# A fused attention and gated-MLP kernel whose instruction order is rehearsed: counting only whole operands for a shared port, with the table of places searched anew

## The chip, the cores and the metric

The kernel runs on one core of one Trainium2 chip. The metric is the device time of one execution in microseconds (us); lower is better. The median of several executions is compared with that of the other kernel.

## What is computed

Eight batches, each with eight attention heads over 576 positions of width 64, and behind them one gated MLP per batch (model width 512, inner width 1024).

```python
scores = 0.125 * q @ k.T
keep   = scores >= max(scores) - tau          # per row
attn   = where(keep, exp(scores - max), 0);  attn /= sum(attn) + 1e-9
x      = heads side by side of attn @ v       # (8, 576, 512)
h      = gelu_tanh(x @ w_in);  u, v = halves of h
v_n    = layer_norm(v) * g_ln
v_s    = einsum('ts,bsd->btd', w_sg, v_n) + b_sg
out    = x + (u * v_s) @ w_out
```

## The kernel before, in words

The heads are handled two at a time. A "pair" n (0 to 31, four to a batch) has nine score tiles of 128 rows by 576 columns: tiles i = 0 to 3 for each head h, and one tile (i = 4, buffer `pm`) that holds the last 64 rows of both heads. Products that need float32 accuracy are made of two parts in a 22-bit format, a high part and a rest, so a score tile is four matmuls against `ks` (high) and `klz` (rest) with `qst`.

For each score tile the engines work in a chain. TensorE writes the scores to PSUM (L785; L767 for the first pair), VectorE takes the negated row maximum (L794, `nm`), GpSimd makes the threshold from it (L800, one column), ScalarE the exponentials (L820, `p`), VectorE then selects and sums (L827: one instruction that reads the scores from PSUM, the threshold column and `p`), TensorE transposes `p` (L535) and ScalarE places the result (L905, L924). The product with `v` is L935. A batch's four pairs give `x`, and only then its MLP matmuls (all of them L1035) can run. They are fed by ScalarE, VectorE and GpSimd through GELU, statistics (L1101, L1104) and splits (L1136, L1196); at the end GpSimd adds the residual (L1223) and SyncE stores.

The weights `w_in` and `w_out` arrive as float64 and are made float32 on the chip, in twelve blocks of 128 rows by 512 columns. A block is loaded by SyncE (L564, `raw_wi` or `raw_wo`, 512 KB), and then takes one ScalarE operation (L572), five VectorE operations (L577, L579, L581, L583, L589) on scratch tiles `wt` or `wz`, and GpSimd and ScalarE operations (L591, L595, L598). These five are called *weight operations* below; there are 60 of them. Blocks `wi01` to `wi31` are the half of `w_in` that the first MLP matmuls need.

SyncE's queue carries all transfers, in order: loads of q, k and v (`rq`, `rk`, `rv`), the weights, and the copies inside SBUF that put a pair's parts in their places (`qst`, L724; `ks`, L702; `klz`, L710; the two `ks` tiles of a pair are `ks<n>_0` and `ks<n>_1`).

The order of all this isn't written by hand. The kernel's body runs twice. The first time it runs against a `Planner` that only records each operation with its engine, an assumed duration and its needs. Each step has a place, `time + scale * OFF[kind] + START[group]`, and `order()` rehearses the program: on each engine, of the steps that could start within `LOOK[engine]` ns of the earliest, the one with the lowest place is taken. The order so found is then issued on the chip, where it is fixed for each engine. One rule of the rehearsal concerns a port that VectorE and GpSimd share: a VectorE operation that is recorded with more than one port (`ports > 1`) starts only after GpSimd's running operation, and holds GpSimd back until it ends itself. These are the lines of it:

```python
if e == "vector" and ops[k][5]:
    if turn["gpsimd"] < start < free["gpsimd"]:
        start = free["gpsimd"]
    turn[e] = start + ns
elif e == "gpsimd":
    start = turn[e] = max(start, turn["vector"])
```

Of the kernel before, what the change touches and what calls it, by code (L numbers as in the profile page):

```python
# [30 lines left out]


OFF = dict(
    tau=-3286.52, q_tails=4436.42, w_load=9629.26, w_abs=4070.14, w_word=-12546.53, w_mul=9713.12, w_add=1259.24,
    w_hi=13076.7, w_lo=-3653.97, w_cast=-4392.8, w_rest=-5913.28, w_place=-8284.37, q_load=4520.75, q_scale=-2406.12,
    q_hi=2053.6, q_lo=-14065.23, q_place=6174.73, q_place_lo=-1344.24, k_load=6900.96, k_hi=430.25, k_lo=10089.47,
    k_place0=9510.54, k_place1=-7562.99, l_place0=-1744.14, l_place1=-1468.81, v_load=11820.02, s=-2160.62,
    nm=5825.84, thr=3055.12, exp=-6580.43, stt=4998.09, t=5700.02, hi=-2640.78, rep=2476.92, tt=119.62, thi=-10085.17,
    guard=-514.64, recip=-6412.4, irep=3638.48, turn=710.41, inv=7549.47, pv=8049.18, rmul=-8520.37, xh=533.49,
    xl=-6641.52, pe=8140.36, msq=-6600.8, stt1=-3927.08, tanh=5227.1, stt2=-2470.89, bn=-4656.45, ag=-8321.5,  # L40
    var=7088.56, rstd=-389.91, shift=3242.69, vn=-2579.53, z=5969.97, zh=-13084.52, zl=-1807.31, mg=-2328.37,
    mgh=3292.78, mgl=454.79, mo=-5098.92, mxl=6386.64, mxh=-6162.46, mst=-19677.21, mlow=-1641.06, madd=5763.85,
    xt=-6497.96,
)
START = {
# [10 lines left out]
}  # L56
LAST_SCALE, SIGMA, SPREAD = 0.55, 1.155, 0.7
LOOK = dict(tensor=20.8, vector=91.4, scalar=115.7, gpsimd=100.2, sync=4015.6)

# [13 lines left out]
    tensor=dict(tensor=0, vector=196, scalar=197, gpsimd=224, sync=190),  # L73
    vector=dict(tensor=230, vector=127, scalar=128, gpsimd=155, sync=120),
    scalar=dict(tensor=260, vector=146, scalar=153, gpsimd=170, sync=135),
    gpsimd=dict(tensor=205, vector=68, scalar=68, gpsimd=100, sync=67),
    sync=dict(tensor=1180, vector=907, scalar=978, gpsimd=983, sync=900),
# [8 lines left out]
def time_of(engine, op, out, args):  # L86

    n = out.size // out.shape[0]
    pointers = sum(a.size == a.shape[0] for a in args) if n > 1 else 0
    args = args or [out]  # L90
    half = out.shape[0] < P and n < 512
    if op == "memset":
        return n / 1.2 + (175 if engine == "gpsimd" and half else 35)
    if engine == "tensor":
        passes = 2 if op == "transpose" else 4 if args[0].dtype == F32 else 1
        beside = 0.5 if min(out.shape[0], args[0].shape[0]) < P and n < 512 else 1.0
        return n * passes * beside / (CLOCK if passes > 1 else STREAM) + (2 if beside == 1 else 20)
    if engine == "scalar":
        return n / 1.2 + (51 if args[0].psum else 93) + 93 * pointers + 115 * half
    if engine == "vector":  # L100
        fast = op == "tensor_scalar" and not args[0].psum
        if op == "tensor_reduce":
            n = args[0].size // args[0].shape[0]
        elif op == "bn_stats":
            n = args[0].size // args[0].shape[0]
        return n / (1.92 if fast else 0.96) + 69 + (60 if pointers else 0)
    if engine == "gpsimd":
        if n == 1 and op == "tensor_tensor":
            return 464 if pointers else 150
        if len(out.shape) == 4:  # L110
            return 149 + n + 140
        return 149 + n * (1.0 if op == "tensor_scalar" else 2.103) + (115 if half or 1 < n < 8 else 0)
    if out.tile.dram:
        return out.size * 0.44
    return out.size * (4 if n >= P else 8) / DMA_BYTES
# [52 lines left out]
class Planner:  # L168
# [51 lines left out]
    def _record(self, engine, op, out, args, accum_out, kw):  # L220
        reads = [a for a in (*args, *kw.values()) if isinstance(a, View)]
        writes = [a for a in (out, accum_out) if isinstance(a, View)]
        me, needs = len(self.ops), {}

        def touch(t):
            self.before[self.current].add(t.step)
            if t.ring:
                ring, k, bufs = t.ring
                if k >= bufs:
                    self.replaced.append((needs, ring[k - bufs]))  # L230

        done = []
        for view, write in [(v, False) for v in reads] + [(v, True) for v in writes]:
            t, (p0, p1, cols) = view.tile, view.area()
            found, rest = False, []
            for j, other, q0, q1, c in t.past:
                meets = q0 < p1 and p0 < q1 and c & cols
                if meets and (write or other) and j != me:
                    found = True
                    needs[j] = needs.get(j, False) or not write  # L240
                if not (write and p0 <= q0 and q1 <= p1 and not c & ~cols and self.ops[j][0] != self.current):
                    rest.append((j, other, q0, q1, c))
            if not found:
                touch(t)
            t.past = rest
            done.append((t, (me, write, p0, p1, cols)))
        for t, entry in done:
            t.past.append(entry)
            t.users[me] = True
        first = writes[0] if writes else reads[0]  # L250
        ports = sum(not a.psum for a in reads) + (op == "tensor_scalar" and not reads[0].psum)
        self.ops.append((self.current, engine, time_of(engine, op, first, reads), needs,
                         P if engine == "tensor" else first.shape[0], engine == "vector" and ports > 1,
                         engine == "tensor" and op != "transpose" and args[0].dtype == F32
                         and min(first.shape[0], args[0].shape[0]) < P))
# [26 lines left out]
    def order(self):  # L282
# [86 lines left out]
        def choose(e):  # L369
# [7 lines left out]
            if starts:  # L377
                soonest = min(starts.values()) + LOOK[e]
                i = min((i for i, t in starts.items() if t <= soonest), key=lambda i: (self.place[i], i))
# [926 lines left out]
```

## Time and profile before

| | |
|---|---|
| median of 3 runs (lowest, highest) | 1009.51 us (1008.3, 1011.13) |
| profiled execution: time, span from first to last instruction | 1008.32 us, 1006.5 us |
| TensorE matmul busy | 966.0 us, 96% of the span |
| VectorE, ScalarE, GpSimd busy | 670.3, 694.3, 622.1 us |
| mean granted TensorE clock | 0.989 |
| moved by DMA | 96.43 MB, mean 96 GB/s |

The page's second part cuts the span into 40 slices of about 25 us. TensorE's digits there begin with 5, 6, 8, 8 and are 9 from the fifth slice to the last but one; VectorE's are 6, 8, 9, 9, 9 in the first five and mostly 6 or 7 after that. A row's "busy" time is the union of its instructions; successive instructions of one engine overlap a little in the records, so that start-to-start distances are shorter than durations. A bracket at the end of a timeline row gives the idle time of the engine before it and what ended it.

### The profile page before, as it was taken

To read this page: it belongs to the slowest core of one execution; us is meant where nothing else is said; L and a number is where in the kernel's file an instruction comes from. 1 tells how busy PE (TensorE), PEld (TensorE's weight loads), DVE (VectorE), ACT (ScalarE), POOL (GpSimd) and SP (SyncE) were. 2 spreads that over 40 slices of the span, in tenths; PEclk is the share of its full clock that TensorE was granted. 3 is DMA by queue.
4 is the path that set the end of the run, shared out by engine and by line. 5 is a ranking of instruction groups with operands and counts; after the bars stand their busy time and mean duration, and the time that the engine had idled before them with its cause. 6 is when DMAs were issued, how large, how long until landed. Compare 5 with 4: busy or idle time off the path is not lost.

```text
span 1006.5 us, 20067 instructions
## 1 busy us (share of the span) xinstructions
PE 966.0 (96%) x6940; PEld 834.5 (83%) x6940; DVE 670.3 (67%) x1419; ACT 694.3 (69%) x1485; POOL 622.1 (62%) x1109
## 2 busy tenths in 40 slices
PE   5688999999999999999999999999999999999997
PEld 4566778898798978889788987889878897889887
DVE  6899988674777657674677746777386755674251
ACT  4678888675778568674786747776577756875362
POOL 4678788557655576555764567555765557634557
PEclk9789999999999999999999999999999999999999
DMA  7855444243134522344133540355223451220001
GB/s 218 252 146 142 114 107 111 67 119 97 43 96 117 140 56 77 94 122 122 32 95 89 143 112 21 87 131 128 80 53 97 113 134 55 71 52 24 24 1 48
DMA packets 50759, 96.43 MB, mean 96 GB/s; under 512 B 8033, under 2 KB 16225, under 8 KB 50658
## 3 DMA queue, kind: packets, MB, share of 16 engines
q1 hardware_dynamic: 50658, 95.15, 35.8%
q8 instruction: 55, 0.90, 0.4%
q14 instruction: 46, 0.38, 0.1%
HBM read 38.44 MB, written 9.44 MB: 48 GB/s over the span
## 4 chain that ended last, share of the span: by engine, by line
PE 70%; POOL 9%; ACT 7%; DMA 5%; DVE 4%; issue 3%; SPq 1%; POOLq 0%; ACTq 0%; DVEq 0%
PE all_banks L1035 35%; PE all_banks L785 13%; PE all_banks L535 11%; PE all_banks L935 11%; POOL z L1136 2%; POOL vv L1123 2%; ACT pt L905 1%; ACT vv L1120 1%; DVE p L827 1%; POOL bn L1112 1%; DMA wt<-in_w_sgT 1%; ACT z L1129 1%; POOL x L953 1%; DMA qst<-qhi 1%; ACT p L820 1%
## 5 line engine op out<-in xcount | busy, mean ns | idle before, releaser
L794 DVE TENSOR_REDUCE nm<-all_banks 128x1 f32<-128x576 f32 x288 | 215.1, 752 | 74.6 <-PE all_banks L785 63.0
L827 DVE SCALAR_TENSOR_TENSOR p<-all_banks,nm,p 128x576 f32<-128x576 f32 x256 | 205.3, 813 | 74.0 <-POOL nm L800 42.5
L820 ACT ACTIVATE p<-all_banks,nm 128x576 f32<-128x576 f32 x256 | 188.2, 744 | 31.3 <-DVE nm L794 30.1
L785 PE MATMUL all_banks<-ks,qst 128*128 128x288 f32 x620 | 189.2, 323 | 8.9 <-DMA ks<-khi 5.1
L905 ACT ACTIVATE pt<-all_banks 128x512 f32<-128x512 f32 (+1 forms) x320 | 169.2, 557 | 24.2 <-PE all_banks L535 22.5
L535 PE MATMUL all_banks<-ident_r,p 128*128 128x128 f32 x1152 | 174.8, 281 | 11.4 <-DVE p L827 8.9
L785 PE MATMUL all_banks<-klz,qst 128*128 128x288 f32 x620 | 174.1, 298 | 0.1
L535 PEld LDWEIGHTS all_banks<-ident_r,p 128*128 128x128 f32 x1152 | 138.1, 144 | 26.5 <-DVE p L827 12.5
L785 PEld LDWEIGHTS all_banks<-ks,qst 128*128 128x128 f32 x620 | 118.3, 191 | 36.0 <-issue 16.9
L935 PE MATMUL all_banks<-pt,rv 128*64 128x320 f32 (+1 forms) x1024 | 138.3, 412 | 0.2
L1035 PE MATMUL all_banks<-x,wi 128*128 128x288 f32 (+2 forms) x768 | 120.4, 299 | 0.0
L785 PEld LDWEIGHTS all_banks<-klz,qst 128*128 128x128 f32 x620 | 118.9, 192 | 1.4 <-DMA klz<-rk 0.6
L800 POOL TENSOR_TENSOR nm<-columns,nm 128x1 f32<-128x1 f32 x288 | 60.5, 217 | 91.3 <-DVE nm L794 87.0
L1035 PE MATMUL all_banks<-wsh,z 128*128 128x288 f32 (+2 forms) x512 | 115.2, 300 | 0.3 <-ACT z L1129 0.3
L1223 POOL TENSOR_TENSOR ot<-ot,x 128x288 f32<-128x288 f32 (+2 forms) x128 | 102.6, 806 | 14.4 <-ACT ot L1220 9.2
L1035 PE MATMUL all_banks<-gh,wo 128*128 128x288 f32 (+2 forms) x512 | 111.5, 300 | 0.0
L1035 PE MATMUL all_banks<-wi,x 128*128 128x512 f32 x448 | 109.3, 393 | 0.4 <-DVE uu L1014 0.4
L935 PEld LDWEIGHTS all_banks<-pt,rv 128*64 128x64 f32 x1024 | 67.8, 136 | 50.4 <-issue 8.2
L1035 PEld LDWEIGHTS all_banks<-x,wi 128*128 128x128 f32 x768 | 106.2, 188 | 0.8 <-issue 0.5
L1035 PEld LDWEIGHTS all_banks<-wi,x 128*128 128x128 f32 x448 | 80.2, 184 | 18.1 <-DVE uu L1014 0.8
L1035 PEld LDWEIGHTS all_banks<-wsh,z 128*128 128x128 f32 x512 | 85.0, 188 | 0.6 <-ACT z L1129 0.5
L1196 POOL TENSOR_TENSOR gl<-uu,gh 128x288 fp32r<-128x288 f32 (+2 forms) x64 | 51.2, 804 | 54.2 <-ACT gh L1192 53.5
(169 smaller groups left out, 1731.3 us busy)
## 6 DMA issues: line engine op xcount, KB each, us to landing
rk<-in_kT SPq DMA_DIRECT2D x32, 320.0 KB, 3.1
rv<-in_vP SPq DMA_DIRECT2D x32, 320.0 KB, 3.0
ks<-khi SPq DMA_DIRECT2D x62, 160.0 KB, 2.6
rq<-in_qT SPq DMA_DIRECT2D x32, 288.0 KB, 3.1
qst<-qhi SPq DMA_DIRECT2D x62, 144.0 KB, 3.2
qst<-rq SPq DMA_DIRECT2D x62, 144.0 KB, 2.4
ks<-khi SPq DMA_DIRECT2D x62, 144.0 KB, 2.5
out_T<-ot SPq DMA_DIRECT2D x56, 144.0 KB, 1.8
```

Of the source, the lines that this page charges most:

```text
L535: nc.tensor.transpose(out, x, ident_r.bitcast(F32))
L785: nc.tensor.matmul(sc[:, a, 0:HALF], w, x, start=(j == 0), stop=(j == len(terms) - 1))
L794: nc.vector.tensor_reduce(nmax, st["s", h, i][:, :, 0:HALF], AX.XY, ALU.max, negate=True)
L800: nc.gpsimd.tensor_tensor(thr, toff, st["nm", h, i], ALU.subtract)
L820: nc.scalar.activation(target(h, i), st["s", h, i][:, :, 0:HALF], AF.Exp, bias=st["nm", h, i])
L827: nc.vector.scalar_tensor_tensor(dst, st["s", h, i][:, :, 0:HALF], st["thr", h, i], dst, ALU.is_ge, ALU.mult, accum_out=st["l", p][:, c:c ...
L905: nc.scalar.activation(dst, src, AF.Copy)
L935: nc.tensor.matmul(acc[h * D:(h + 1) * D, 0:w], st["v"][:, o:o + D], unit(h, p)[:, kt, 0:w] if kt < NM else tail_unit(p)[:, 0:w], start=(k ...
L1035: nc.tensor.matmul(st["acc"][0:rows[0]] if rows else st["acc"], w, x, start=(j == 0), stop=(j == n - 1))
L1123: nc.gpsimd.tensor_tensor(st["v", i], st["v", i], g_bc[0:rows], ALU.mult)
L1196: nc.gpsimd.tensor_tensor(st["gl", p, d], st["u", p, d], st["gh", p, d], ALU.subtract)
L1223: return lambda: nc.gpsimd.tensor_tensor(o(), o(), x[b, m][:, ts_], ALU.add)
```

## The change

Three things are edited. The line that counts an operation's SBUF operands for the port now leaves out operands of one element per partition (columns such as a threshold). By the old line the select (L827: threshold column and `p` from SBUF) counted two ports, by the new one it counts one. The weight operations, and the GELU operations of a batch's last 64 rows (L1014, L1020), count two by either. The numbers in `OFF`, `START` and `LOOK` are all replaced; `LOOK` for SyncE goes from 4015.6 to 49883.6 ns, for GpSimd from 100.2 to 250.5, for TensorE from 20.8 to 109.7. No operation is added, removed or resized.

```diff
-    tau=-3286.52, q_tails=4436.42, w_load=9629.26, w_abs=4070.14, w_word=-12546.53, w_mul=9713.12, w_add=1259.24,
...
+    tau=-13072.53, q_tails=17013.18, w_load=24017.7, w_abs=10671.59, w_word=11608.84, w_mul=22204.76, w_add=6419.5,
...
-LOOK = dict(tensor=20.8, vector=91.4, scalar=115.7, gpsimd=100.2, sync=4015.6)
+LOOK = dict(tensor=109.7, vector=84.7, scalar=108.3, gpsimd=250.5, sync=49883.6)
...
-        ports = sum(not a.psum for a in reads) + (op == "tensor_scalar" and not reads[0].psum)
+        ports = sum(not a.psum and a.size > a.shape[0] for a in reads) + (op == "tensor_scalar" and not reads[0].psum)
```

What this moves is seen in the built programs. Names carry the pair and the tile (`p4_0` is `p` of pair 4, tile 0) and a serial number that differs between the two.

SyncE's queue in the opening, before: the stretch that ends in the copies for pair 1's second `ks` tile.

```order
L685 DMA rk2_265<-in_kT 128x640
L564 DMA raw_wi30_272<-in_w_in 128x1024
L564 DMA raw_wi01_281<-in_w_in 128x1024
L564 DMA raw_wi11_288<-in_w_in 128x1024
L564 DMA raw_wi21_292<-in_w_in 128x1024
L564 DMA raw_wi31_297<-in_w_in 128x1024
L564 DMA raw_wo0_311<-in_w_out 128x1024
L564 DMA raw_wo1_313<-in_w_out 128x1024
L564 DMA raw_wo2_320<-in_w_out 128x1024
L702 DMA ks1_1_338<-khi1_228 64x640 x2
```

The same engine after the change, the stretch up to the same copies.

```order
L564 DMA raw_wi30_156<-in_w_in 128x1024
L724 DMA qst01_115<-qhi1_162 64x576
L724 DMA qst11_117<-qhi1_162 64x576
L724 DMA qst01_115<-rq1_138 64x576
L724 DMA qst11_117<-rq1_138 64x576
L702 DMA ks1_0_243<-khi1_231 64x576 x2
L710 DMA klz10_124<-rk1_143 64x640
L685 DMA rq2_268<-in_qT 128x576
L710 DMA klz01_123<-rk1_143 64x576
L702 DMA ks1_1_296<-khi1_231 64x640 x2
L685 DMA rk2_315<-in_kT 128x640
```

In the first, eleven of the twelve weight loads stand ahead of `ks1_1` in the queue (three of them ahead of the rows shown); in the second four do, and `rv0` and `rv1`, which stood ahead, now follow.

VectorE in the opening, before: from the first select of pair 1's tile 0 to the next maxima of its second head.

```order
L827 SCALAR_TENSOR_TENSOR p1_0_370,l1_0_371<-all_banks_91,nm1_0_0_363,p1_0_370 128x576
L579 TENSOR_SCALAR wz0_349<-wz0_349 128x512
L794 TENSOR_REDUCE nm1_0_1_410<-all_banks_91 128x1
L843 RECIPROCAL l0_1_277<-l0_1_277 128x5
L581 SCALAR_TENSOR_TENSOR wz0_349<-raw_wi01_281,wz0_349 128x512
L589 SCALAR_TENSOR_TENSOR wt3l_245<-raw_wi20_183,wt3l_245 128x512
L577 TENSOR_SCALAR wt4h_422<-wt4h_422 128x512
L583 TENSOR_SCALAR wz0_349<-wz0_349 128x512
L579 TENSOR_SCALAR wt4h_422<-wt4h_422 128x512
L827 SCALAR_TENSOR_TENSOR p1_1_419,l1_0_371<-all_banks_91,nm1_0_1_410,p1_1_419 128x576
L581 SCALAR_TENSOR_TENSOR wt4h_422<-raw_wi30_272,wt4h_422 128x512
L794 TENSOR_REDUCE nm1_1_0_455<-all_banks_91 128x1
```

VectorE after the change, from the same select on.

```order
L827 SCALAR_TENSOR_TENSOR p1_0_355,l1_0_356<-all_banks_91,nm1_0_0_337,p1_0_355 128x576
L843 RECIPROCAL l0_1_261<-l0_1_261 128x5
L827 SCALAR_TENSOR_TENSOR p1_0_355,l1_0_356<-all_banks_91,nm1_1_0_374,p1_0_355 128x576
L946 TENSOR_TENSOR x32_0_0_408<-all_banks_91,ir0_0_238 128x256
L794 TENSOR_REDUCE nm1_0_1_417<-all_banks_91 128x1
L583 TENSOR_SCALAR wt3l_205<-wt3h_204 128x512
L579 TENSOR_SCALAR wt4h_376<-wt4h_376 128x512
L589 SCALAR_TENSOR_TENSOR wt3l_205<-raw_wi20_153,wt3l_205 128x512
L794 TENSOR_REDUCE nm1_0_2_447<-all_banks_91 128x1
L794 TENSOR_REDUCE nm1_1_1_459<-all_banks_91 128x1
L827 SCALAR_TENSOR_TENSOR p1_1_453,l1_0_356<-all_banks_91,nm1_0_1_417,p1_1_453 128x576
```

The weight operations that stood between the two selects of that tile have moved behind them. Counted from the programs' starts, 52 weight operations stand ahead of the second select of pair 4's tile 0 before and 46 after, with 38 selects and 39 maxima ahead in both; up to the last select of pair 3's tile 3 it is 51 and 44.

TensorE around the transposes of pair 4's tile 0, before.

```order
L535 MATMUL all_banks_91<-ident_r_92,p4_0_1177 128x128 x4
L535 MATMUL all_banks_91<-ident_r_92,ir3_1_1219 128x128 x2
L535 MATMUL all_banks_91<-ident_r_92,l3_1_1060 128x128
L785 MATMUL all_banks_91<-ks4_1_1087,qst10_116 128x288
L785 MATMUL all_banks_91<-klz10_124,qst10_116 128x288
L785 MATMUL all_banks_91<-ks4_1_1087,qst10_116 128x288
L785 MATMUL all_banks_91<-klz10_124,qst10_116 128x288
L535 MATMUL all_banks_91<-ident_r_92,p4_0_1177 128x128 x5
```

TensorE after the change, at the same place.

```order
L1035 MATMUL all_banks_91<-wi11_1069,x1_693 128x512 x3
L1035 MATMUL all_banks_91<-wi21_1159,x2_942 128x512 x2
L785 MATMUL all_banks_91<-ks4_1_1108,qst10_116 128x288
L785 MATMUL all_banks_91<-klz10_124,qst10_116 128x288
L785 MATMUL all_banks_91<-ks4_1_1108,qst10_116 128x288
L785 MATMUL all_banks_91<-klz10_124,qst10_116 128x288
L1035 MATMUL all_banks_91<-wi21_1159,x2_942 128x512
L1035 MATMUL all_banks_91<-wi31_1168,x3_1184 128x512 x3
L535 MATMUL all_banks_91<-ident_r_92,p4_0_1143 128x128
L535 MATMUL all_banks_91<-ident_r_92,ir3_1_1239 128x128 x2
L535 MATMUL all_banks_91<-ident_r_92,l3_1_1052 128x128
L535 MATMUL all_banks_91<-ident_r_92,p4_0_1143 128x128 x4
```

Twelve MLP matmuls of the first batch (three stand just ahead of the rows shown) now come before the second half of these transposes; before, the first of them comes some 50 rows after these.

More of the change, by code (lines that the diff above doesn't have):

```diff
@@ L33 @@
 OFF = dict(
-    tau=-3286.52, q_tails=4436.42, w_load=9629.26, w_abs=4070.14, w_word=-12546.53, w_mul=9713.12, w_add=1259.24,
[L35 to L43, printed above, removed]
+    tau=-13072.53, q_tails=17013.18, w_load=24017.7, w_abs=10671.59, w_word=11608.84, w_mul=22204.76, w_add=6419.5,
+    w_hi=10498.51, w_lo=-13326.63, w_cast=9980.35, w_rest=-4899.43, w_place=-2267.44, q_load=4326.97, q_scale=4377.77,
+    q_hi=-2442.43, q_lo=-12231.14, q_place=30436.83, q_place_lo=1664.62, k_load=10334.3, k_hi=-6857.66, k_lo=-685.55,
+    k_place0=-19333.51, k_place1=-3297.61, l_place0=24572.89, l_place1=-14784.81, v_load=58431.42, s=-30373.95,
+    nm=13996.8, thr=-3490.07, exp=18012.16, stt=18418.78, t=-1553.44, hi=6288.69, rep=20685.74, tt=-6558.4,
+    thi=2889.11, guard=-2787.69, recip=-3700.6, irep=-995.86, turn=-5627.14, inv=30071.87, pv=18033.85,
+    rmul=-18400.62, xh=12547.41, xl=-45570.85, pe=4060.27, msq=-202.81, stt1=19882.23, tanh=-4905.84, stt2=-19666.94,
+    bn=-16580.9, ag=-14071.83, var=-3342.04, rstd=21481.31, shift=19191.57, vn=5742.16, z=15012.34, zh=-12985.82,
+    zl=-11826.14, mg=-6619.76, mgh=23319.86, mgl=-3933.56, mo=20106.66, mxl=28163.49, mxh=-20280.11, mst=-31173.79,
+    mlow=-19270.9, madd=8715.79, xt=-19524.59,
 )
 START = {
[10 rows of a table removed]
[10 rows of a table added]
 }
 LAST_SCALE, SIGMA, SPREAD = 0.55, 1.155, 0.7
-LOOK = dict(tensor=20.8, vector=91.4, scalar=115.7, gpsimd=100.2, sync=4015.6)
+LOOK = dict(tensor=109.7, vector=84.7, scalar=108.3, gpsimd=250.5, sync=49883.6)
 WHOLE_SCORES = 1
```

20 rows, old and new, of the table START are left out of this document.

## The prediction

> **What bounds the kernel now.** I read the page's slices first, then busy time by stretch, then TensorE's waits, then the rows at the end of the stretch that loses. By stretch (us in all, then each engine's busy us and count; the last three are the granted clock, the DMA share and GB/s):
>
> ```profile
> core 0: us, PE busy (x) PEld busy (x) DVE busy (x) ACT busy (x) POOL busy (x), PEclk, DMA share, GB/s
> 0.00:111.10 111.10, 81.66 (x503) 62.49 (x504) 95.80 (x190) 76.89 (x154) 74.45 (x124) 0.91 0.65 185
> 111.10:150.00 38.90, 37.35 (x259) 28.60 (x258) 33.15 (x71) 32.88 (x70) 31.20 (x53) 1.00 0.42 106
> 150.00:950.00 800.00, 796.77 (x5844) 696.22 (x5843) 522.13 (x1123) 559.33 (x1212) 478.65 (x885) 1.00 0.34 88
> 950.00:1006.50 56.50, 50.24 (x339) 47.23 (x337) 19.20 (x40) 25.15 (x52) 37.85 (x51) 0.99 0.07 24
> ```
>
> TensorE is idle 29.4 us in the first 111, 1.6 in the next 39, 3.2 in the 800 of the middle and 6.3 at the end. Since no operation is added or removed, only idle time (and time at a lower clock) can be won, nearly all of it ahead of 111 us. What TensorE waits for there (in 0 to 150 us: total, times, longest), and the two ends of VectorE's stretch:
>
> ```profile
> PE all_banks L535 <- DVE p L827: 10.5, 10, 2.7
> PE all_banks L785 <- DMA ks<-khi: 5.1, 1, 5.1
> ...
> 8.94 1.42 DVE L794 TENSOR_REDUCE nm<-all_banks 128x1 f32<-128x576 f32 x2 [4.49 <-PE all_banks L767]
> 110.31 0.81 DVE L827 SCALAR_TENSOR_TENSOR p<-all_banks,nm,p 128x576 f32<-128x576 f32 x1
> ...
> 111.31 0.71 PE L535 MATMUL all_banks<-ident_r,p 128*128 128x128 f32 x5
> ...
> 8.90:111.10 102.20, 79.40 (x496) 60.65 (x494) 95.10 (x184) 74.93 (x152) 67.58 (x103) 0.90 0.65 184
> ```
>
> The longest total is the wait for the select. The select of pair 4's tile 0 ends at 111.1 and its transposes start at 111.3: TensorE follows VectorE, which is busy 95.1 of the 102.2 us from its first maximum to that point and idle 7.1. So the opening is as long as VectorE's queue up to there: work, port waits and idle time. Past it the MLP gives TensorE work that needs VectorE less. What shortens that queue, or gives TensorE other work ahead of it, moves the end one for one.
>
> **The change part by part.** *The count of ports* alone changes nothing on the chip; it changes what the rehearsal believes. Select durations in min/median/max ns, then a weight operation beside a GpSimd operation (start and duration, us), then two weight operations alone:
>
> ```profile
> L827 DVE SCALAR_TENSOR_TENSOR p<-all_banks,nm,p x256: 784/815/820, 10.6 to 917.5; 128x576 f32<-128x576 f32 x128
> ...
> 48.46 1.69 DVE L579 TENSOR_SCALAR wz<-wz 128x512 uint32<-128x512 uint32 x1
> 48.31 1.54 POOL L695 TENSOR_TENSOR rk<-rk,khi 128x640 fp32r<-128x640 f32 x1 [1.26 <-ACT khi L691]
> L579 DVE TENSOR_SCALAR wt13h<-wt13h x1: 422/422/422, 91.6 to 91.6; 128x512 uint32<-128x512 uint32 x1
> L581 DVE SCALAR_TENSOR_TENSOR wt4h<-raw_wi,wt4h x1: 681/681/681, 42.4 to 42.4; 128x512 uint32<-128x512 uint32 x1
> ```
>
> 256 selects never exceed 820 ns whatever GpSimd does, so the old count was wrong for them; the weight operation ends 0.30 us after GpSimd's does (50.15 against 49.85), 1.27 us late. The new rehearsal charges the wait where the chip has it.
>
> *VectorE's order.* Ahead of pair 4's tile 0 stand 46 weight operations in place of 52: one L577, one L579, two L581, two L583 fewer. At 0.42 us (0.68 for L581 and L589), the durations alone, that is 3.0 us less. TensorE also has twelve MLP matmuls ahead of these transposes; a row of twelve:
>
> ```profile
> 963.46 2.91 PE L1035 MATMUL all_banks<-wi,x 128*128 128x512 f32 x12
> ...
> 107.80 0.74 PE L535 MATMUL all_banks<-ident_r,p 128*128 128x128 f32 x5 [0.58 <-DVE p L827]
> 110.38 0.44 PE L535 MATMUL all_banks<-ident_r,ir 128*128 128x128 f32 x2 [0.68 <-POOL ir L850]
> ```
>
> 2.9 us of work that no longer follows. The place just ahead, pair 3's tile 3 (the row at 107.80), gains less and so decides: 44 weight operations for 51 (one L577, one L579, three L581, three L583 fewer, one L589 more), 3.5 us less, and one select of 0.82 more: 2.6. Between the two places the kernel before loses another 0.68 at 110.38, which the twelve matmuls would cover. **3.3 us** (ends: 2.6 and 5.9, the sum at the later place).
>
> *SyncE's order.* The copies of `ks1_1` no longer queue behind seven loads of 512 KB (the last row: KB each, median us from issue to landing):
>
> ```profile
> 42.65 0.58 PE L785 MATMUL all_banks<-ks,qst 128*128 128x288 f32 x1 [5.06 <-DMA ks<-khi]
> 36.77 0.76 DVE L794 TENSOR_REDUCE nm<-all_banks 128x1 f32<-128x576 f32 x1 [1.92 <-PE all_banks L785]
> 43.98 0.76 DVE L794 TENSOR_REDUCE nm<-all_banks 128x1 f32<-128x576 f32 x1 [0.94 <-PE all_banks L785]
> ...
> raw_wi<-in_w_in SPq DMA_DIRECT2D x8, 512.0 KB, 8.2
> ```
>
> At 258 GB/s (row of 32.5 us below) 3.67 MB take 14.2 us, more than the 5.06 that TensorE waits. But VectorE had weight operations meanwhile and idled only 1.92 and 0.94: **2.8 us** (ends: 0 if another idle stretch takes their place, 5.1 the whole wait). What is moved the other way, two weight loads ahead of `qst` and the two `rv` loads behind, is 0.39 MB more ahead of `qst`, 1.5 us at that rate. I cost it at nothing, since `qst` landed at 16.25 and was first read at 28.32:
>
> ```profile
> 7.94 8.31 DMA qst<-qhi
> 28.32 0.38 PE L785 MATMUL all_banks<-ks,qst 128*128 128x288 f32 x1
> ```
>
> If the first read comes so much sooner that this cover of 12 us is gone, it costs the 1.5. `rv0`, now behind `ks1_1`, is first read only after pair 0's last transposes; if it is late there, its 320 KB cost about 1 us.
>
> *The port wait.* Busy us of L577, L579, L581, L583 and L589, in that order, in the same 102.2 us:
>
> ```profile
> 8.90:111.10 102.20, 6.87 (x11) 0.90 0.65 184
> 8.90:111.10 102.20, 8.00 (x11) 0.90 0.65 184
> 8.90:111.10 102.20, 11.31 (x11) 0.90 0.65 184
> 8.90:111.10 102.20, 7.64 (x11) 0.90 0.65 184
> 8.90:111.10 102.20, 5.42 (x9) 0.90 0.65 184
> ```
>
> Alone the first four would take 11 x (0.42 + 0.42 + 0.68 + 0.42) = 21.3; they take 33.8, so 12.5 us are waits for the port, and L589 shows none. A rehearsal that sees the true collisions can place operations around some of them; how many no trace of before shows. Ends: 12.5 gained (all gone) and 6 lost (below). I take a quarter, **3.0 us**, nearer to no change, since a rehearsal with assumed durations is off by some tenths of a us after tens of us.
>
> *The middle and the end.* TensorE's idle 3.2 us in 800 is the most that the middle can give; new places, and TensorE's wider look of 0.11 us, can also cost. I take 0 (ends: 3 gained, 3 lost). The last four output units come one after the other in both orders, so the tail stays: 0.
>
> Sum against the profiled execution, 1008.3: 1008.3 - 3.3 - 2.8 - 3.0 = **999.2 us**. The median shown is 1.2 above it, within the spread of its three runs; a run over 0.3% from it (3 us) can be told from no change, so faster means under 1006.5.
>
> **Rivals.** *The clock stays full.* Stretches with a clock of one half:
>
> ```profile
> 32.50:46.20 13.70, 7.55 (x32) 6.94 (x32) 10.76 (x21) 9.97 (x21) 8.22 (x8) 0.50 0.81 258
> 56.40:59.80 3.40, 3.13 (x14) 3.01 (x14) 3.40 (x10) 2.10 (x5) 2.01 (x5) 0.50 0.96 274
> 66.60:70.10 3.50, 3.50 (x18) 3.44 (x16) 3.01 (x7) 2.65 (x6) 1.85 (x5) 0.51 0.50 175
> ```
>
> TensorE is busy 14.2 us there, so 7.1 would be saved if no such stretch were left and TensorE were the bound. My sum takes none of it, since VectorE is 79 to 100% busy in them. If scores that come sooner also end VectorE's idle time, the time is 999.2 - 7.1 = 992.1. For it: the longest stretch holds the 5.06 us wait that falls. The Trainium skill ("TensorE: Matmul & The Clock Gate", section "What's actually happening") says that TensorE is throttled by default and that activity releases it; the trace agrees so far, its low clocks all stand among idle gaps.
>
> *The collisions vanish:* 12.5 in place of 3.0, 989.7. Against it: GpSimd is busy 67.6 of the 102.2 us, so gaps for 44 operations are few.
>
> *The collisions are drawn anew.* If weight operations fall at random beside GpSimd, with its share of 0.66 and half of a long operation, each waits 0.66 x 0.64 = 0.42 us:
>
> ```profile
> L598 POOL TENSOR_TENSOR wi<-wz,wi 128x512 fp32r<-128x512 f32 x4 | 5.1, 1280 | 0.1
> ```
>
> 44 of them wait 18.6 us, 6 more than now, and 3.3 + 2.8 - 6.1 leaves 1008.3: no change. For it: an order that fits its rehearsal can miss on the chip. The Trainium skill ("SBUF — State Buffer", section "Who interferes with whom") states that whoever starts first holds the shared pair for the whole instruction and the other fully blocks; the row at 48.46 agrees. By that rule with random starts this rival's 1008.3 would be the forecast, by the trace's own 12.5 us, kept, it is 1002.2.
>
> *A wait in the repeated batches: slower.* SyncE now goes by places alone within 50 us, so a copy that must wait can hold a load behind it. The chain already passes through two such landings in the middle, which cost TensorE nothing:
>
> ```profile
> 449.69 4.10 DMA rk<-in_kT
> 510.89 4.30 DMA klz<-rk
> ```
>
> Such a landing left bare once in each of seven batches costs 7 x 4.2 = 29 us: 999.2 + 29 = 1028. It decides from (9.1 + 3) / 7 = 1.7 us a batch on. Against it: before's queue does the same, and TensorE stays 99.6% busy.
>
> *Nothing gained, since the order is the same* is excluded: the three places shown differ.
>
> **How the numbers follow.** Forecast 0.60 (its own range 994 to 1003, from the larger and smaller ends of the first two terms), clock 0.12, collisions gone 0.09, drawn anew 0.11, slower 0.08. Faster 0.60 + 0.12 + 0.09 = 0.81, same 0.11, slower 0.08. The range runs from 989.5, which holds the collisions-gone case, to 1007, which holds part of the drawn-anew case; some 0.15 is left out.
>
> **What would show it.** TensorE's idle time ahead of the fifth pair's first transposes falls from 29 to some 20 us. The 5.06 us wait at `ks1_1` is gone or under 1 us. The four L577 to L583 groups sum to some 9 us above their own time, for 12.5. Middle and end stay at 3 and 6 us idle. I am wrong if VectorE's idle time ahead of that point grows past 7.1 us (another transfer, or scores that come late), if the weight groups are longer than now, or if the middle's TensorE share falls below 99%.

## The result: slower by 0.6%, and the profile after

The changed kernel takes 1015.1 us (median; 1010.7 to 1017.6) against 1008.4 us for the kernel before beside it: a ratio of 1.0061, with a 95% interval of 1.0043 to 1.0079. 999.2 us had been forecast. The profiled execution took 1015.8 us, its span is 1014.0.

By stretch, after (columns as in the prediction's first fence):

```profile
0.00:111.10 111.10, 85.74 (x543) 64.25 (x544) 91.23 (x194) 81.19 (x167) 78.29 (x131) 0.95 0.66 189
111.10:150.00 38.90, 38.00 (x271) 30.16 (x270) 36.76 (x76) 33.27 (x69) 32.65 (x56) 1.00 0.41 102
150.00:950.00 800.00, 787.85 (x5746) 683.32 (x5745) 507.00 (x1105) 551.86 (x1194) 472.76 (x868) 1.00 0.34 87
950.00:1014.00 64.00, 56.97 (x386) 52.12 (x384) 22.99 (x46) 27.72 (x57) 42.22 (x56) 0.99 0.08 26
```

The same rows tell both halves of the story, by the number of TensorE's instructions (both kernels have 6940). At 150 us it stands at 543 + 271 = 814 where the kernel before had 762: 52 more, and at 137 ns each (800 us for 5844 in the prediction's row) that is a lead of 7.1 us. Weighted by what each kind of instruction takes, it is about 9 us. In the 800 us behind that, it does 5746 where the kernel before did 5844: 98 fewer, 13.4 us. The opening gains most of the 9.1 us forecast, and the repeated batches lose nearly twice as much.

In the middle, TensorE's idle time goes from 3.2 to 12.2 us. Its waits between 250 and 850 us (total, times, longest), before (there are only two) and then after, the longest three:

```profile
PE all_banks L785 <- DVE p L827: 1.8, 6, 0.3
PE all_banks L785 <- ACT tt L924: 0.4, 1, 0.4
```

```profile
PE all_banks L535 <- ACT tt L924: 4.0, 5, 0.8
PE all_banks L535 <- POOL ir L850: 1.9, 3, 1.0
PE all_banks L535 <- DVE p L827: 1.6, 2, 1.4
```

No wait is long. One of 0.8 us comes once in every batch, and a few of other kinds with it. The weight loads, which TensorE makes ahead of its matmuls, show where most of the loss sits. Their wait for GpSimd's L850 (it writes `ir`, the reciprocals that TensorE then transposes) in the same 600 us, before and then after, and one such place in the changed kernel:

```profile
PEld all_banks L535 <- POOL ir L850: 1.5, 5, 0.3
```

```profile
PEld all_banks L535 <- POOL ir L850: 9.7, 16, 1.3
...
724.37 0.27 POOL L1116 TENSOR_SCALAR bn<-bn 128x1 f32<-128x1 f32 x1
724.71 1.28 POOL L1136 TENSOR_TENSOR z<-vv,z 128x512 fp32r<-128x512 f32 x1
725.96 0.41 POOL L850 TENSOR_SCALAR ir<-l 128x256 f32<-128x256 f32 x1
...
726.02 0.39 ACT L924 ACTIVATE tt<-all_banks 128x64 f32<-128x64 f32 x2
...
726.56 0.41 PE L535 MATMUL all_banks<-ident_r,ir 128*128 128x128 f32 x2 [0.81 <-ACT tt L924]
```

GpSimd comes to L850 without idle time from other work, here the MLP's, and TensorE, whose order is fixed, stands still. ScalarE's copy (L924) ends within 0.1 us of L850 here, so two engines are late together. Counted from the start of one matmul to the start of the next, the transposes of `ir` take 226 ns each in the middle where they took 131. There are 106 of them, so that is 10.1 us, most of the 13.4 lost.

The length of a batch is read from the starts of VectorE's row maxima (L794, 36 to a batch): the 145th and the 253rd are three batches apart. Before, then after:

```profile
442.20 0.76 DVE L794 TENSOR_REDUCE nm<-all_banks 128x1 f32<-128x576 f32 x1 [0.29 <-PE all_banks L785]
...
799.33 0.76 DVE L794 TENSOR_REDUCE nm<-all_banks 128x1 f32<-128x576 f32 x1 [0.29 <-PE all_banks L785]
```

```profile
439.57 0.76 DVE L794 TENSOR_REDUCE nm<-all_banks 128x1 f32<-128x576 f32 x1 [0.43 <-PE all_banks L785]
...
803.00 0.76 DVE L794 TENSOR_REDUCE nm<-all_banks 128x1 f32<-128x576 f32 x1 [0.43 <-PE all_banks L785]
```

A batch takes 357.1 / 3 = 119.0 us before and 363.4 / 3 = 121.1 after. The page's fourth part, the chain of work that ended last by its share of the span, says what kind of loss this is. Before, then after:

```profile
PE 70%; POOL 9%; ACT 7%; DMA 5%; DVE 4%; issue 3%; SPq 1%; POOLq 0%; ACTq 0%; DVEq 0%
```

```profile
PE 47%; POOL 16%; ACT 12%; DVE 9%; DMA 9%; issue 6%; SPq 1%; POOLq 0%; ACTq 0%; DVEq 0%
```

TensorE is 96% busy in both kernels, but it carries 70% of the chain in the one and 47% in the other. More than half of the time of the changed kernel is set by work on the other engines and by transfers. Below, such a line of work is called a ring, since it comes back in every batch. A stretch of it in one batch of the changed kernel, the pieces over 0.1 us (start and duration in us):

```profile
742.51 0.31 ACT x L951
...
742.89 0.74 POOL x L953
743.63 0.15 POOL nm L800
743.78 0.16 POOL bn L1108
...
744.01 0.56 POOL bn L1112
...
744.67 0.28 POOL bn L1116
...
744.97 0.82 ACT vv L1120
...
745.87 1.29 POOL vv L1123
...
747.18 0.65 ACT z L1129
...
747.90 1.30 POOL z L1136
```

Nothing in this stretch waits for TensorE: each piece starts within 0.1 us of the end of the one above. A piece of such a ring that is late can lengthen the batch; by how much, the runs below show.

### The profile page after: what moved, and what is told of

Same layout as the page of the kernel before. It is cut to its first block, busy times and chain, and to the rows that moved or that the text cites. A ratio compares the mean times of both kernels' runs of the same rounds, so it can differ in the third digit from the quotient of the medians.

```text
span 1014.0 us, 20062 instructions
## 1 busy us (share of the span) xinstructions
PE 968.6 (96%) x6940; PEld 829.9 (82%) x6940; DVE 658.0 (65%) x1419; ACT 694.0 (68%) x1485; POOL 625.9 (62%) x1109
## 4 chain that ended last, share of the span: by engine, by line
PE 47%; POOL 16%; ACT 12%; DVE 9%; DMA 9%; issue 6%; SPq 1%; POOLq 0%; ACTq 0%; DVEq 0%
PE all_banks L1035 26%; PE all_banks L785 9%; PE all_banks L535 7%; PE all_banks L935 4%; DVE p L827 3%; ACT pt L905 3%; POOL vv L1123 3%; POOL x L953 2%; DMA qst<-qhi 2%; DMA ks<-khi 2%; POOL ot L1223 2%; ACT p L820 2%; POOL z L1136 2%; DMA rq<-in_qT 2%; ACT vv L1120 2%
## 5 line engine op out<-in xcount | busy, mean ns | idle before, releaser
L827 DVE SCALAR_TENSOR_TENSOR p<-all_banks,nm,p 128x576 f32<-128x576 f32 x256 | 205.6, 812 | 83.4 <-ACT p L820 39.4
L794 DVE TENSOR_REDUCE nm<-all_banks 128x1 f32<-128x576 f32 x288 | 211.6, 750 | 55.5 <-PE all_banks L785 43.9
L785 PE MATMUL all_banks<-ks,qst 128*128 128x288 f32 x620 | 185.5, 318 | 9.3 <-DVE p L827 4.8
L905 ACT ACTIVATE pt<-all_banks 128x512 f32<-128x512 f32 (+1 forms) x320 | 164.6, 561 | 16.3 <-PE all_banks L535 14.0
L535 PE MATMUL all_banks<-ident_r,p 128*128 128x128 f32 x1152 | 165.8, 277 | 7.7 <-DVE p L827 6.4
L785 PE MATMUL all_banks<-klz,qst 128*128 128x288 f32 x620 | 172.0, 296 | 0.0
L535 PEld LDWEIGHTS all_banks<-ident_r,p 128*128 128x128 f32 x1152 | 134.1, 143 | 25.9 <-DVE p L827 10.2
L800 POOL TENSOR_TENSOR nm<-columns,nm 128x1 f32<-128x1 f32 x288 | 59.4, 211 | 119.2 <-DVE nm L794 107.9
L1035 PE MATMUL all_banks<-x,wi 128*128 128x288 f32 (+2 forms) x768 | 117.8, 300 | 1.2 <-DVE x L946 1.2
L785 PEld LDWEIGHTS all_banks<-klz,qst 128*128 128x128 f32 x620 | 117.8, 190 | 0.7
L1035 PE MATMUL all_banks<-wi,x 128*128 128x512 f32 x448 | 112.3, 395 | 0.5 <-DVE uu L1014 0.5
L1035 PEld LDWEIGHTS all_banks<-gh,wo 128*128 128x128 f32 x512 | 83.9, 188 | 0.6 <-ACT pt L905 0.3
```

The costliest lines, as they stand in the source:

```text
L535: nc.tensor.transpose(out, x, ident_r.bitcast(F32))
L785: nc.tensor.matmul(sc[:, a, 0:HALF], w, x, start=(j == 0), stop=(j == len(terms) - 1))
L794: nc.vector.tensor_reduce(nmax, st["s", h, i][:, :, 0:HALF], AX.XY, ALU.max, negate=True)
L800: nc.gpsimd.tensor_tensor(thr, toff, st["nm", h, i], ALU.subtract)
L827: nc.vector.scalar_tensor_tensor(dst, st["s", h, i][:, :, 0:HALF], st["thr", h, i], dst, ALU.is_ge, ALU.mult, accum_out=st["l", p][:, c:c ...
L905: nc.scalar.activation(dst, src, AF.Copy)
```

## The experiments

Their times are compared through the ratio to the kernel before that ran beside them. In the table, "0-230" and "230-820" are TensorE's instructions in these stretches (us), and the batch is taken from L794 as above. The numbers quoted from the expectations were counted with batches of 121.1 to 121.3 us (after) and 118.6 to 119.0 (before). Counts and batches are those of one profiled execution; in a_short, a_less and c_prices it took 2.3, 3.5 and 2.9 us less than the median, in a_oldlook 2.9 more.

| run | us | ratio (95% interval) | 0-230 | 230-820 | batch, us |
|---|---|---|---|---|---|
| before | 1008.4 | 1 | 1355 | 4309 | 119.0 |
| after | 1015.1 | 1.0061 (1.0043 to 1.0079) | 1403 | 4227 | 121.1 |
| hyb_ab | 1009.5 | 1.0014 (1.0003 to 1.0025) | 1349 | 4303 | 119.2 |
| hyb_ab198 | 1002.2 | 0.9941 (0.9927 to 0.9955) | 1405 | 4298 | 119.3 |
| hyb_ba | 1026.5 | 1.0181 (1.0165 to 1.0197) | 1327 | 4221 | 121.5 |
| a_mult | 1007.8 | 0.9997 (0.9985 to 1.0009) | 1413 | 4269 | 120.1 |
| b_mult | 1002.0 | 0.9938 (0.9923 to 0.9953) | 1353 | 4344 | 118.1 |
| a_short | 1011.2 | 1.0032 (1.0020 to 1.0044) | 1417 | 4261 | 120.8 |
| b_short | 1005.9 | 0.9978 (0.9970 to 0.9987) | 1366 | 4317 | 118.7 |
| a_both | 1001.7 | 0.9940 (0.9927 to 0.9954) | 1410 | 4302 | 119.5 |
| b_both | 999.1 | 0.9922 (0.9910 to 0.9934) | 1379 | 4354 | 117.8 |
| a_less | 1010.6 | 1.0018 (1.0003 to 1.0033) | 1406 | 4154 | 120.9 |
| b_less | 995.6 | 0.9867 (0.9848 to 0.9886) | 1365 | 4260 | 117.2 |
| b_newrule | 1040.7 | 1.0322 (1.0298 to 1.0347) | 1283 | 4160 | 122.3 |
| a_oldlook | 1037.8 | 1.0289 (1.0266 to 1.0312) | 1325 | 4139 | 124.1 |
| c_prices | 1006.2 | 0.9985 (0.9973 to 0.9998) | 1407 | 4287 | 119.4 |

**Which part of the order loses: mixed orders.** A list of steps stands in the kernel in place of what its rehearsal finds. It is made of the first part of one order and the rest of the other.

```diff
-    order = planner.order()
+    order = [int(i) for i in ORDER.split()]
```

> The steps that the new order begins in its first 100 us stay in the new order (615 of 5547), and all the rest stands in the order of the kernel before; banks are assigned by the rehearsal along that sequence. Theory (the opening gains about 9 us and keeps them, the middle of the new order loses them): a batch in the middle takes 118.5-119 us and the whole 997-1004. Rival (an opening that ends earlier is given back whatever the order behind it): 1006-1012.

Half of it: 119.2 us a batch, before's pace, but 1009.5 us in all. The lead is lost where the orders meet. In the same count as above, TensorE does 231 instructions between 111 and 150 us, where the kernel before did 259:

```profile
111.00:150.00 39.00, 32.21 (x231) 24.30 (x231) 32.55 (x70) 28.70 (x63) 25.71 (x46) 1.00 0.37 96
```

> As the first mixed kernel, with the seam put later: 1244 of 5547 steps stand in the new order (those that it plans to begin in its first 198 us, the whole first batch and a part of the second), the rest in the order of before. The first mixed kernel kept the pace of before in the middle but lost some 5.6 us of TensorE's time at its seam, between 111 and 150 us. Theory: the new order's lead (about 7 us of work at 200 us) is now carried through, a batch behind it takes 118.5-119 us, and the whole 998-1003. Rival (whatever is gained early is lost where the orders meet): 1006-1010.

With a better seam the theory holds: 1002.2 us, faster than both kernels. Its rows show the new opening (1405 against 1355) with nearly the old middle (4298 against 4309):

```profile
0.00:230.00 230.00, 202.15 (x1405) 165.90 (x1406) 182.15 (x388) 170.04 (x357) 162.75 (x277) 0.97 0.53 145
230.00:820.00 590.00, 587.00 (x4298) 510.34 (x4297) 392.51 (x844) 420.20 (x905) 352.07 (x660) 1.00 0.37 94
```

> The reverse: the steps that the order of before begins in its first 100 us stay in that order (525), and all the rest stands in the new order. Theory: it has the slow opening and the slow middle, a batch of 121-122 us and a whole of 1020-1027. Rival (the opening decides nothing, the rest alone does): 1013-1017, as the changed kernel.

1026.5 us and 121.5 us a batch, as the theory had it. The slow middle belongs to the new order of the middle. It comes whatever stands ahead of it, and goes with it. So does the wait of the weight loads for L850 (250 to 850 us): 9.1 us in hyb_ba, 1.5 in hyb_ab198.

**What a batch is bound by: less work for TensorE.**

```diff
                 for j in range(lo, hi):
+                    if j == SKIP and name[0] in "uyo" and name[1] in "123456":
+                        continue
                     w, x, *rows = term(j)
```

> The changed kernel with its order and banks as they are; in the batches 1 to 6 each product of the names u, y and o leaves out one of its 12 or 14 matmuls (24 a batch; those terms are missing from the sums). 24 matmuls of about 133 ns are 3.2 us of TensorE a batch. Theory (a batch of the new order is set by a ring of waits through all five engines, of which TensorE is less than half): little of it is seen, a batch falls from 121.1 us by 0.3-1.2 us and the whole from 1015 to 1008-1013. Rival (TensorE sets the batch and its gaps are only added to it): a batch falls by 2.5-3.2 us and the whole to 996-1001.

> The same matmuls left out of the kernel before. Theory: its batch is TensorE's for two thirds, with its ring of waits close behind, so it falls from 118.9 us by more than that of the changed kernel, 0.8-1.8 us, and the whole to 996-1003. Rival (TensorE alone sets it): by 2.5-3.2 us, the whole 989-993.

19 us of TensorE's work (144 matmuls of 133 ns) is taken out of both. The kernel before turns seven tenths of it into time (1.33%, 13.4 us, just past the theory's range; 1.8 a batch), the changed kernel less than a quarter (0.43%, 4.3 us; 0.2 a batch in the three counted). Three batches are few: over five (the 73rd to the 253rd row maximum) it is 1.6 a batch against 0.8. So TensorE mostly sets the batch of the one, and hardly that of the other. In the chain of a_less its share is lower still:

```profile
PE 43%; POOL 16%; ACT 13%; DVE 13%; DMA 7%; issue 7%; SPq 1%; POOLq 0%; ACTq 0%; DVEq 0%
```

The Trainium skill ("Perfetto Trace Analysis", section "Optimization Strategies") advises to keep the matmul engine as highly utilized as possible and, where it idles, to optimize the engines that block the critical path. By the second half the trace agrees; the first alone would have missed this case, where 96% and 96% hide the difference.

**What the rehearsal did not see: two prices.** In `time_of`, the duration that the rehearsal assumes for a one-column operation of two tensors on GpSimd is always 150 ns, since `pointers` is 0 where `n` is 1:

```python
pointers = sum(a.size == a.shape[0] for a in args) if n > 1 else 0
...
if n == 1 and op == "tensor_tensor":
    return 464 if pointers else 150
```

The reciprocal root of the layer norm (L1112) is such an operation, and stands in the ring shown above with 0.56 us. Line L1112 in the changed kernel and in a_mult (duration in ns, min/median/max):

```profile
L1112 POOL TENSOR_TENSOR bn<-bn,columns x40: 542/555/892, 112.3 to 981.8; 128x1 f32<-128x1 f32 x32, 64x1 f32<-64x1 f32 x8
```

```profile
L1112 POOL TENSOR_TENSOR bn<-bn,columns x40: 182/191/517, 110.6 to 973.1; 128x1 f32<-128x1 f32 x32, 64x1 f32<-64x1 f32 x8
```

```diff
-                nc.gpsimd.tensor_tensor(t[:, 8:9], t[:, 8:9], mhalf[0:rows], ALU.pow)
+                nc.gpsimd.tensor_tensor(t[:, 8:9], t[:, 8:9], mhalf[0:rows], ALU.mult)
```

> The changed kernel with its order and banks as they are; only the one-column operation of L1112 on GpSimd is a multiplication where it was a reciprocal root (the root is left out). Theory: the rehearsal prices this operation at 150 ns, the trace shows about 550, and in the new order its lateness (some 0.4 us, five times a batch) reaches TensorE, so a batch in the middle falls from 121.3 us to about 119.3 and the whole from 1015 to 1001-1007. Rival (the waits of the middle come from loads and stores that are late, or from the places themselves): a batch stays at 121.0-121.5 us and the whole at 1012-1016.

> The same edit on the kernel before, as a control (the root is left out here too). Theory: its order has slack at that place, so a batch stays at 118.3-118.7 us and the whole at 1005-1009. Rival: the root's time costs every order alike, and this kernel too falls by more than 5 us, below 1003.

My theory falls here in half. The root does cost the changed kernel 0.64% (6.5 us), but the kernel before has no slack for it either: 0.62% (6.2 us), the rival's number. It delays both orders alike and does not explain their difference. The five roots of a batch are shortened by 1.8 us together (0.36 each), and a batch falls by 1.0 and 0.9 us: about half of the lateness counted.

The second price is that of transfers; by how much the rehearsal has it wrong, no row here shows. Copies were shortened to 64 columns (the lines left out keep the second head's keys in one tile):

```diff
-                    nc.sync.dma_start(q[h][r0:r0 + D, h * TAIL:h * TAIL + S].bitcast(F32),
-                                      st[name][h * D:(h + 1) * D, :S].bitcast(F32))
+                    w = S if n < 4 else CUT
+                    nc.sync.dma_start(q[h][r0:r0 + D, h * TAIL:h * TAIL + w].bitcast(F32),
+                                      st[name][h * D:(h + 1) * D, :w].bitcast(F32))
...
-                    nc.sync.dma_start(st["ks", h][d0:d0 + D].bitcast(F32),
+                    nc.sync.dma_start(st["ks", h][d0:d0 + D, 0:w].bitcast(F32),
```

> The changed kernel with its order and banks as they are; from the second batch on, the copies of the queries (L724) and of the second head's keys (L702) within SBUF move the first 64 columns alone, so that they land earlier; the other columns keep old values (that part of the work is left out). Theory (the new order leaves no slack for transfers that land a few tenths of a us later than its rehearsal supposes, along the ring copy of the queries, conversion into the one buffer hi, copy of the keys): a batch falls from 121.3 us to 119.3-120.0 and the whole to 1003-1008. Rival (the middle's loss lies in the compute engines' order alone): a batch stays at 121.0-121.5 and the whole at 1012-1016.

> The same shorter copies in the kernel before, as a control (the same part of the work is left out). Theory: its order has slack for these transfers, a batch stays at 118.4-118.7 us and the whole at 1005-1009. Rival (earlier copies help every order): below 1003.

The copies of the queries land 0.6 us sooner (KB each, median us from issue to landing, between 250 and 850 us; the changed kernel, then a_short):

```profile
qst<-qhi SPq DMA_DIRECT2D x40, 144.0 KB, 2.4
```

```profile
qst<-qhi SPq DMA_DIRECT2D x40, 16.0 KB, 1.8
```

The middle gains 34 instructions after and 8 before, the direction of the theory, but the batch falls by some 0.3 us in both and not by 1.3 or more. In the whole the two kernels gain about alike (0.29% and 0.22%). Neither price alone makes the difference.

> The changed kernel, order and banks kept, with both edits at once: L1112 multiplies (the root is left out), and the copies of L724 and L702 move 64 columns from the second batch on (the others keep old values). Theory (these two late links are most of what the ring loses): a batch of 119.0-119.8 us, the whole 999-1004. Rival (other links of the ring are as late): 120.0-120.5 us a batch, the whole 1005-1009.

> The same two edits at once in the kernel before (the same parts left out). Both views expect little beyond what the root alone gave (1002.0): a batch of 117.9-118.2 us and the whole 998-1002.

Both at once: the changed kernel falls by 1.21% (12 us), more than the two edits singly would add up to (0.93%), and the kernel before by 0.78%, about their sum (0.84%). The excess of 0.28% is no larger than the uncertainty of the four ratios together, so it does not show that one link hides the other. The difference between the orders falls from 0.61% to 0.18%, about 4 us of 6. In the middle itself it falls much less: a batch of the changed kernel was 2.1 us longer than the other's and is still 1.7 longer; the deficit falls from 82 instructions to 52, the lead at 230 us from 48 to 31 (the kernel before gains there too), and the rest is won behind 820 us. The weight loads' wait for L850 falls from 9.7 to 5.1 us and is not gone.

**A search with the prices mended.** `OFF`, `START` and `LOOK` were searched on from the new tables. The search rehearsed with the durations that the next paragraph lists, with some smaller ones mended too (by up to 45 ns, or 1.5% of a long GpSimd operation), and weighed in a case where transfers land 450 ns later; the order found stands in the kernel as a list (the edit of the mixed orders), so the prices themselves stand nowhere in it.

> A new order: the changed kernel's rule, with OFF, START and LOOK searched on from its tables, by its own rehearsal with the prices set to what the trace of the changed kernel shows (the root of L1112 557 ns instead of 150, L1108 175 instead of 150, L1116 224 instead of 150, L850 371 instead of 545, the selects 740 instead of 729, and every transfer landing 0.25 us later), nothing else changed; the order found stands in the kernel as a list. Theory (the middle was lost to a rehearsal that knows no such delays, and so leaves no slack for them): a batch takes 118-119 us, the opening keeps its lead, and the whole is 990-1000. Rival (what the middle loses is nothing that these prices hold): a batch of 120 us or more and a whole of 1003 or more.

119.4 us a batch, and the lead of the opening is there (1407 instructions by 230 us). Of the middle's deficit of 82 instructions 22 are left. But 1006.2 us in all misses the forecast by 6 us and falls on the rival's side. (Its profiled execution, at 1003.3, is the lowest of twelve that reach to 1009.8, so its rows flatter it.) It is 0.76% faster than the changed kernel, hardly faster than the one before (0.15%), and slower than the mixed order, for which nothing was searched. The weight loads' wait for L850 is down to 0.8 us. What the prices did in this isn't shown: no order was searched on as long with the old prices, and the search alone may have found the better middle.

**The change in parts.**

```diff
-        ports = sum(not a.psum for a in reads) + (op == "tensor_scalar" and not reads[0].psum)
+        ports = sum(not a.psum and a.size > a.shape[0] for a in reads) + (op == "tensor_scalar" and not reads[0].psum)
```

> The rule alone: the kernel before, its tables OFF, START and LOOK unchanged, with the new count of port operands (and so another order wherever the rehearsal now times differently). Theory (tables fit only the rehearsal they were searched with): slower than both, 1018-1040. Rival (the old rule's charge was the whole fault, and taking it away brings the opening's gain by itself): 998-1003.

```diff
-LOOK = dict(tensor=109.7, vector=84.7, scalar=108.3, gpsimd=250.5, sync=49883.6)
+LOOK = dict(tensor=20.8, vector=91.4, scalar=115.7, gpsimd=100.2, sync=4015.6)
```

> One part undone: the changed kernel, its rule, OFF and START, with LOOK as it was (SyncE's 49883 ns back to 4015, GpSimd's 250 to 100, TensorE's 110 to 21). Theory (the tables are of one piece): slower than the changed kernel, 1018-1040. Rival (the rigid order of the transfers, which SyncE's large LOOK gives, costs the middle its 2.5 us a batch): a batch returns to 118.5-119 us and the whole to 998-1006.

1040.7 and 1037.8 us, both some 3% slower than before, and the batch of a_oldlook grows to 124.1: taking SyncE's rigid order away, with all that the rehearsal then moves, does not bring the middle back. All five values of `LOOK` are undone there, so SyncE's alone is not tested. A truer rule with tables fitted to the old one is worse than either whole.

## Why the prediction was wrong, point by point

- *What bounds the kernel* was read from busy shares: idle time can only be won ahead of 111 us. That bounds the gain rightly. It does not bound a loss, and the row that speaks of losses, the chain with TensorE at 70%, was not read: 30% of the time of the kernel before was already set by other engines and transfers. The two landings that the prediction put at nothing were read off this very chain.
- *The opening's terms* sum to 9.1; the lead at 150 us is 7.1 by count and about 9 by work, and the mixed order that keeps it ends 0.59% (5.9 us) ahead of the kernel before. The sum is near by luck, for its parts are not: the second select of pair 4's tile 0, the point that the sum was to bring 9.1 us forward, ends at 106.0 us instead of 111.1, 5.1 earlier. VectorE is busy 85.5 of the 97.1 us from its first maximum to there, 9.6 us less than before, but it is idle 11.7 us there instead of 7.1. That is one of the signs of being wrong that the prediction named.
- *SyncE's order* did at its place what was forecast. The copies of `ks1_1` are issued at 23.8 and 24.3 us and land within 2.7 us, no longer 12 to 14, and the first matmul that reads them, at 28.32, shows no wait. But TensorE waits again further on, at the third tile of that head, for a select that follows 1.79 us of VectorE's own waiting. The term's lower end, another idle stretch in its place, came in great part:

```profile
28.32 0.40 PE L785 MATMUL all_banks<-ks,qst 128*128 128x288 f32 x1
...
39.04 0.82 DVE L827 SCALAR_TENSOR_TENSOR p<-all_banks,nm,p 128x576 f32<-128x576 f32 x1 [1.79 <-ACT p L820]
39.92 0.61 PE L785 MATMUL all_banks<-ks,qst 128*128 128x288 f32 x1 [3.54 <-DVE p L827]
```

- *The port wait* was sized too small. Busy time of L577, L579, L581, L583 and L589 between 8.9 and 111.1 us, after:

```profile
8.90:111.10 102.20, 4.10 (x10) 0.95 0.66 186
8.90:111.10 102.20, 5.75 (x10) 0.95 0.66 186
8.90:111.10 102.20, 7.01 (x10) 0.95 0.66 186
8.90:111.10 102.20, 5.29 (x9) 0.95 0.66 186
8.90:111.10 102.20, 7.87 (x8) 0.95 0.66 186
```

  The first four sum to 22.2 us; alone they would take 29 x 0.42 + 10 x 0.68 = 19.0. So 3.2 us of waits are left of 12.5 (I expected some 9), and 2.4 have come to L589 (7.87 - 8 x 0.68). That is 6.9 us fewer, not 3.0; VectorE's idle time took back 4.6.
- *Idle time ahead of 111 us* falls from 29.4 to 25.4, not to 20. Part of the rest of the gain is clock. These are the stretches at half the clock, after:

```profile
39.60:43.00 3.40, 3.08 (x13) 3.06 (x14) 3.13 (x8) 2.72 (x7) 3.29 (x5) 0.50 0.87 220
53.20:60.10 6.90, 5.99 (x25) 3.37 (x26) 3.51 (x9) 3.90 (x8) 5.17 (x6) 0.51 0.74 219
```

  TensorE is busy 9.1 us in them, where it was 14.2; by the prediction's own working, half of the difference, 2.6 us, is saved. With 4.0 us less idle time ahead of 111 us and 0.7 less behind it, this makes 7.3, close to the lead by count. The rival "the clock stays full" is true in part.
- *The middle and the end: 0 (ends 3 gained, 3 lost)* is the step that failed. The middle lost 13.4 us by count, 9.0 of it as idle time and most of it at the transposes of `ir`. The lower end of 3 had no row behind it. I took the smallness of TensorE's idle time before for a bound on both sides.
- The rival *a wait in the repeated batches* was right in kind, with 0.08: 2.1 us a batch, past the 1.7 from which it was to decide. Its mechanism was not: no wait of TensorE in the middle ends with a landing, though transfers went from 5% to 9% of the chain, and the middle did not come back where `LOOK` was undone. The sign that I named, a middle with TensorE's share below 99%, is there (787.85 of 800, 98.5%).

What is shown: the new order of the middle loses its time whatever stands ahead of it; there, little of the batch is TensorE's; and most of the loss sits at the transposes of `ir`, which wait for GpSimd's L850 and, once a batch, also for ScalarE's copy. The weight loads' wait for L850 is there in both orders with the new middle (9.7 and 9.1 us in 600) and hardly there in the kernel before and hyb_ab198 (1.5) or in the order searched anew (0.8). The root and the long copies, taken away together, account for some 4 of the 6 us between the kernels, but for only 30 of the 82 instructions that the middle loses.

What stays open: the other 52 instructions (7 us), which no run assigns to a price; what the mended prices did in the order that was searched anew; and which of the edits (the count, `OFF`, `START`, `LOOK`) led to this middle, since both runs that split them gave yet another order, some 3% slower. That the old rule's needless charge on the selects had worked as a reserve for such lateness is possible, but it was not tried apart.

## What to carry to other kernels

An idle bound on the busiest engine limits what a new order can win, not what it can lose: read the chain's shares for the loss, and bring a chain that is already 30% elsewhere into the range. Look at the waits of the weight loads too: the rows of TensorE's matmuls gave GpSimd's L850 1.9 us, those of the weight loads 9.7. A searched order may be fitted to its rehearsal's errors, so compare assumed and traced durations line by line before searching, starting with the operations on the chain. When two orders are good in different stretches, splice them, and choose the seam with care: one mixed order lost its lead there, the other cost no search and beat both kernels.

## What was not expected of the hardware

The reciprocal root of one column on GpSimd takes 0.55 us where a multiplication of the same column takes 0.19. A copy of a ninth of the bytes lands in 1.8 us instead of 2.4: most of the time is not the bytes'. The Trainium skill ("DMA: Bandwidth & Descriptors", section "Anatomy of one DMA — SWDGE (gpsimd) path") gives a transfer that GpSimd issues a fixed cost of about 2.0 us besides its bytes. These copies are issued by SyncE, so their 1.8 us is near that figure but no test of it; no run here has a transfer of the other kind.
